# Gate and value products of the second expert by seven half-block products in fp16, in two passes over the tokens

## The chip, the cores and the metric

One core of a Trainium2 chip runs the whole program. The metric is device time in microseconds (us) of one execution, the median over executions. TensorE (PE) multiplies, VectorE (DVE), ScalarE (ACT) and GpSimd (POOL) do elementwise work, and the queue of SyncE (SP) issues nearly all DMAs.

## The reference

```python
def _moe2_ref(x, w_gate, w_val, w_out, rms_g):      # x: 2304 x 512
    rms = np.sqrt(np.mean(x * x, axis=-1, keepdims=True) + 1e-06)
    xn = x / rms * rms_g
    g = xn @ w_gate                                  # 512 x 1536
    silu = g * (1.0 / (1.0 + np.exp(-g)))
    val = xn @ w_val                                 # 512 x 1536
    return (silu * val @ w_out).astype(np.float32)   # 1536 x 512
...
attn_out = _attn_ref(**attn_kwargs)                  # block-causal, 4 batches, 8 heads, 576 x 64
x = attn_out.transpose(0, 2, 1, 3).reshape(B * S, H * D)
x = _moe_ref(x=x, **moe_kwargs)                      # softplus(x @ w_in) @ w_out, hidden 2048
return _moe2_ref(x=x, **moe2_kwargs)
```

## The kernel before

The 2304 tokens are cut into six blocks of 384 (`BLK`), features stand on the partitions. Every operand of a large product is held as a high and a low part in fp32r (a four-byte type), and each product is three matmuls (`PASSES`: high-high, high-low, low-high) that add up in one PSUM bank.

The program has three stretches. In the first (to about 406 us) attention runs together with nine of the sixteen hidden tiles of the first expert (`s_tile`, `pv`, `g1`, `g2`). Attention's probabilities are turned by DMA transposes (`pt<-pst`) that the SP queue issues; `pv` multiplies them in fp16. In the second stretch (to about 584 us) the other seven hidden tiles of each block run (`g1`, `g2`, `evac_b`), while the weights of the second expert are prepared. The third stretch is the second expert: 6 blocks by 12 hidden tiles of 128, which the text calls 72 f-steps. `g34` makes the gate and the value tile of one f-step, each from 12 matmuls of 128 x 384; the sigmoid, two multiplications and a split into high and low part follow on ACT and DVE; `g5`, one f-step later, multiplies the result by the output weights, 9 matmuls of 128 x 512. `out2` copies out a finished block, and `load_xn` normalises the next.

Weights come as 64-bit words. `w_unit` loads 512 KB (`wraw`), rebuilds fp32 values in `wa` by two ACT, three DVE and one POOL instruction per half, and splits them into `w`. Eleven of the 18 second-expert units are prepared in the second stretch, seven at the start of the third.

Nothing of the order is written by hand. Each operation is recorded with an engine, a cost, a priority and its cells; `Plan.schedule` simulates the engines, picks the operation with the lowest key among those ready, chooses between engines where `op2` offers several, and the result is emitted as one fixed order per engine. PE records matmuls in the helper `mm` (L422), so groups of PE are told apart by tiles: `b<-x,w` is `g1` or `g34`, `b<-g,w` is `g2`, `b<-w,g` is `g5`.

## Time and profile before

| | |
|---|---|
| time, median of 3 | 1040.66 us (1040.28 to 1041.27) |
| profiled execution's span, first to last instruction | 1038.3 us |
| what lies around the span, against the median | 2.4 us |
| PE busy | 1009.9 us, 97% of the span |
| DVE, ACT, POOL busy | 667.8, 580.1, 214.0 us |
| second expert's products | from about 584 us to 1033.7 us |

The time of the profiled execution itself is not given, so its span is set beside the median. A busy share is an average over the three stretches; the stretches differ, and what an edit is worth is read from its own.

### The profile page before, as it was taken

Reading aid. Unit: us, or ns where it says so; the run is one execution under the profiler, and the core shown is the slowest. Engines: PE = TensorE matmul, PEld = TensorE weight load, DVE = VectorE, ACT = ScalarE, POOL = GpSimd, SP = SyncE. Lnnn points to the kernel's source line nnn. Section 1 sums busy time; section 2 is a strip of 40 time slices with the busy share of each in tenths; the row PEclk is TensorE's granted clock in tenths of the full one; section 3 lists DMA queues with packets and bytes.
Section 4 is the critical chain, followed back from the end, with each engine's and each line's share of the span. In section 5 each row is a group of like instructions: output and inputs, shape, how many; then the busy total and the mean of one; then the engine's idle time right before and its main releaser. Section 6 shows DMA issues by size and latency. Waiting matters only on the chain.

```text
span 1038.3 us, 16885 instructions
## 1 busy us (share of the span) xinstructions
PE 1009.9 (97%) x6136; PEld 941.9 (91%) x6136; DVE 667.8 (64%) x1592; ACT 580.1 (56%) x1352; POOL 214.0 (21%) x289
## 2 busy tenths in 40 slices
PE   5999899999999999999999999999999999999998
PEld 4677898999989999999999999999999999999997
DVE  6899999887888677777888899422422423222322
ACT  6999798777778678877878664211211212111111
POOL 3543433331233023223324342000000000000000
PEclk9999999999999999999999999999999999999999
DMA  7454787958556635456444634200100100000000
GB/s 263 133 194 150 191 196 167 252 116 201 130 132 117 111 102 183 164 209 212 162 158 159 199 102 142 69 1 1 62 1 1 62 1 1 31 1 1 31 1 31
DMA packets 111635, 115.19 MB, mean 111 GB/s; under 512 B 84544, under 2 KB 92352, under 8 KB 110528
## 3 DMA queue, kind: packets, MB, share of 16 engines
q1 hardware_dynamic: 110976, 107.83, 36.8%
q0 software_dynamic: 576, 6.29, 1.6%
q8 instruction: 48, 0.79, 0.3%
q14 instruction: 35, 0.29, 0.1%
HBM read 72.03 MB, written 21.63 MB: 90 GB/s over the span
## 4 chain that ended last, share of the span: by engine, by line
PE 73%; DVE 9%; ACT 8%; DMA 7%; issue 2%; POOL 1%; SPq 0%; POOLq 0%; ACTq 0%; DVEq 0%
PE b L422 73%; DMA pt<-pst 4%; DMA wraw<-in_w_dram 2%; ACT P L661 1%; POOL wa L461 1%; ACT wa L448 1%; DVE wa L456 1%; DVE g L337 1%; ACT w L327 1%; DVE nm L627 1%; DVE wa L458 1%; DVE pst L686 1%; DVE t L836 1%; ACT t L834 1%; ACT P L705 1%
## 5 line engine op out<-in xcount | busy, mean ns | idle before, releaser
L422 PE MATMUL b<-x,w 128*128 128x384 f32 x2880 | 543.6, 338 | 2.0 <-DVE nm L669 0.8
L422 PEld LDWEIGHTS b<-x,w 128*128 128x128 f32 x2880 | 503.8, 188 | 13.8 <-issue 1.3
L422 PE MATMUL b<-g,w 128*128 128x384 f32 x1152 | 229.8, 339 | 2.2 <-DVE g L337 1.9
L422 PEld LDWEIGHTS b<-g,w 128*128 128x128 f32 x1152 | 199.4, 188 | 6.5 <-DVE g L337 3.6
L422 PE MATMUL b<-w,g 128*128 128x512 f32 x648 | 160.4, 392 | 0.0
L932 DVE TENSOR_TENSOR t<-b,t 128x384 f32<-128x384 f32 x72 | 40.0, 556 | 165.3 <-ACT t L931 165.1
L422 PEld LDWEIGHTS b<-w,g 128*128 128x128 f32 x648 | 120.6, 188 | 21.8
L461 POOL TENSOR_TENSOR wa<-wa,wraw 128x512 int32<-128x512 int32 x68 | 95.2, 1401 | 204.0 <-DVE wa L456 119.1
L931 ACT ACTIVATE t<-b 128x384 f32<-128x384 f32 x72 | 35.2, 490 | 171.8 <-PE b L422 171.8
L934 ACT CAST g<-t 128x384 fp32r<-128x384 f32 x72 | 36.8, 513 | 136.4 <-DVE t L933 136.4
L661 ACT ACTIVATE P<-b,nm 128x288 f32<-128x288 f32 (+8 forms) x160 | 80.1, 502 | 16.3 <-DVE nm L639 4.5
L627 DVE TENSOR_REDUCE nm<-b 128x1 f32<-128x288 f32 (+8 forms) x160 | 70.7, 447 | 18.7 <-PE b L422 17.6
L933 DVE TENSOR_TENSOR t<-b,t 128x384 f32<-128x384 f32 x72 | 39.9, 556 | 61.5 <-PE b L422 61.5
L686 DVE SCALAR_TENSOR_TENSOR pst<-P,nm,pst 128x128 f16<-128x128 f32 (+4 forms) x108 | 68.3, 638 | 9.1 <-ACT pst L683 6.7
L422 PE MATMUL b<-khl,qbd 128*128 128x448 f32 (+7 forms) x360 | 68.9, 312 | 1.0 <-ACT pt L722 1.0
L337 DVE TENSOR_TENSOR g<-t,g 128x384 fp32r<-128x384 f32 x96 | 60.5, 632 | 11.4 <-ACT g L327 10.9
L836 DVE SCALAR_TENSOR_TENSOR t<-b,t 128x384 f32<-128x384 f32 x96 | 52.6, 551 | 21.4 <-ACT t L835 21.0
L935 DVE TENSOR_TENSOR g<-t,g 128x384 fp32r<-128x384 f32 x72 | 42.9, 597 | 35.4 <-ACT g L934 35.4
L422 PEld LDWEIGHTS b<-khl,qbd 128*128 128x128 f32 x360 | 57.1, 188 | 3.9 <-ACT pt L722 1.2
L327 ACT CAST g<-t 128x384 fp32r<-128x384 f32 x96 | 49.2, 516 | 19.9 <-DVE t L836 16.8
L448 ACT ACTIVATE wa<-wraw 128x512 f32<-128x512 f32 x68 | 46.1, 678 | 20.9 <-DMA wraw<-in_w2gv_dram 10.7
L833 ACT ACTIVATE t<-b 128x384 f32<-128x384 f32 x96 | 46.5, 493 | 19.1 <-PE b L422 19.0
(91 smaller groups left out, 1055.7 us busy)
## 6 DMA issues: line engine op xcount, KB each, us to landing
wraw<-in_w_dram SPq DMA_DIRECT2D x32, 512.0 KB, 3.6
wraw<-in_w2gv_dram SPq DMA_DIRECT2D x24, 512.0 KB, 3.6
yd<-y SPq DMA_DIRECT2D x12, 768.0 KB, 3.7
y<-yd SPq DMA_DIRECT2D x12, 768.0 KB, 4.5
qf<-in_qP_dram SPq DMA_DIRECT2D x42, 192.0 KB, 2.8
xd<-x SPq DMA_DIRECT2D x4, 1536.0 KB, 7.1
x<-xd POOLq DMA_DIRECT2D x4, 1536.0 KB, 7.4
wraw<-in_w2o_dram SPq DMA_DIRECT2D x12, 512.0 KB, 4.4
```

The costliest lines, as they stand in the source:

```text
L327: "ACT": ("ACT", t_act(n), lambda: nc.scalar.copy(dst(), src())),
L337: "DVE": ("DVE", t_dve(n), lambda: nc.vector.tensor_tensor(dst(), a(), b(), ALU.subtract)),
L422: nc.tensor.matmul(o, lhsT=l, rhs=r, start=start, stop=stop)
L448: op("ACT", t_act(CW), prio, lambda a=a, hv=halves: nc.scalar.activation(a(), hv()[1].bitcast(FP32), ACTF.Abs), [raw], [a])
L461: op("POOL", t_pool2(CW), prio, lambda a=a, hv=halves: nc.gpsimd.tensor_tensor(a().bitcast(I32), a().bitcast(I32), hv()[0].bitcast(I32), A ...
L627: aop("DVE", t_dve(cn), key, lambda sp=sp, col=col, cn=cn: nc.vector.tensor_reduce(nm()[:, col:col + 1], sp()[:, :cn], axis=AX.X, op=ALU.m ...
L661: aop("ACT", 0.24 + cn * 0.836e-3, key, lambda sp=sp, col=col, c0=c0, cn=cn: nc.scalar.activation(P()[:, c0:c0 + cn], sp()[:, :cn], ACTF.E ...
L686: aop("DVE", t_dve(c, True), key, lambda: nc.vector.scalar_tensor_tensor(lo(), pc(), r(), hi(), ALU.mult, ALU.subtract), [P, (P, "pad"), ( ...
L833: op("ACT", t_act(BLK, False), key - 5, lambda: nc.scalar.activation(e(), h()[:, :BLK], ACTF.Abs), [h], [e])
L836: op("DVE", t_dve(BLK), key - 5, lambda: nc.vector.scalar_tensor_tensor(e(), h()[:, :BLK], 0.0, e(), ALU.max, ALU.add), [h, e], [e])
L932: op("DVE", t_dve(BLK), key + 2, lambda: nc.vector.tensor_tensor(u(), ga()[:, :BLK], u(), ALU.mult), [ga, u], [u])
L935: op("DVE", t_dve(BLK), key + 4, lambda: nc.vector.tensor_tensor(g()[:, 1], u(), g()[:, 0].bitcast(FP32), ALU.subtract), [u, (g, 0)], [(g, ...
```

## The change

The gate and value weights of two hidden tiles and the two token halves of a block are taken as two by two blocks: the 512 input features in halves, the 384 tokens in halves of 192 (`HB`). Seven products of sums of blocks (Strassen's scheme) replace the eight of the plain form; all operands are scaled and split into fp16 parts. A pair-step is what two f-steps were: 7 products of 12 matmuls 128 x 192, then 18 output matmuls of 128 x 512. There are 36. Silu is computed in one ACT instruction. Four of six pair-steps of every block run in a first pass (`SPL`), whose sums are stored in DRAM (`acc_dram`) with the seven mixed token blocks (`xn_dram`); a second pass runs the other two and adds. Scales need the largest weight, so `top_unit` loads all weights once more and takes a maximum on DVE: 24 halves of gate and value during attention, 12 of the output weights in the second stretch.

```diff
-    NW2 = NF2 + NF2 // 2
+    HB = 192
+    NP2 = NF2 // 2
+    NW2 = NF2 + NF2 // 4
...
+    def top_unit(i, key, prio):
+        for c in range(2):
+            raw = R_wraw.new()
+            hw = raw_pair(raw)[1]
+            load(prio - 6, raw, w_src[key[0]][key[1], c], writes=[raw], nbytes=128 * CW * 8)
+            op("DVE", t_dve(CW), prio, lambda k=2 * i + c, hw=hw: nc.vector.tensor_reduce(top(k), hw().bitcast(FP32), axis=AX.X, op=ALU.max, apply_absolute_value=True), [raw] + ([fac_b] if i >= NF2 else []), [("tops", 2 * i + c)])
...
+    def split_w(dst, src, n, r, rd, cells, prio):
+
+        op("ACT", t_act(n) + 0.09, prio, lambda: nc.scalar.activation(dst(0), src(), ACTF.Copy, scale=fac(r)), rd, [cells[0]])
+        op("DVE", t_dve(n, True), prio, lambda: nc.vector.scalar_tensor_tensor(dst(1), src(), fac(r), dst(0), ALU.mult, ALU.subtract), rd + [cells[0]], [cells[1]], port=True)
+
+    def gv_unit(f, ring, prio):
...
+        split_w(lambda l: dst(l, 0, 256).rearrange("p (k n) -> p k n", k=2), lambda: gp(0), 256, 0, [(g, 0)] + fc, [(w, 0, 0), (w, 1, 0)], prio)
+        split_w(lambda l: dst(l, 256, 768), lambda: fl()[:, 512:], 512, 0, [(g, 1)] + fc, [(w, 0, 1), (w, 1, 1)], prio)
+        for o, a, b in ((0, 1, 0), (1, 3, 1), (3, 3, 0), (2, 2, 3)):
...
+        split_w(lambda l: dst(l, 768, 1792), fl, 1024, 0, [(g, 0), (g, 1)] + fc, [(w, 0, 2), (w, 1, 2)], prio)
...
+        split_x(2, a22, hi_c, q(3))
+        mix(a22, a21, a22, ALU.add, lo_c + hi_c + q(3), q(3))
+        split_x(0, a11, lo_c, q(0))
+        split_x(3, a22, q(3), q(3))
+        mix(a21, a11, a21, ALU.subtract, lo_c + q(0, 3), q(2))
+        mix(a11, a22, a11, ALU.subtract, q(0, 2, 3), q(0))
+        split_x(1, a12, hi_c, q(1))
+        split_x(5, a21, q(2), q(2))
+        split_x(4, a11, q(0), q(0))
+        mix(a12, a12, a11, ALU.subtract, q(0, 1), q(1))
+        split_x(6, a12, q(1), q(1))
...
-                    for k in (2 * c, 2 * c + 1):
-                        for m, (a, l) in enumerate(PASSES):
-                            mm(o()[:, :BLK], w_view(w)[:, a, (k * 2 + q) * 128:(k * 2 + q + 1) * 128], x()[:, k, l, :], k == 0 and m == 0, k == KD - 1 and m == 2)
...
+                for f in range(2):
+                    for k in range(2):
+                        for m, (a, c) in enumerate(PASSES):
+                            mm(o()[:, HB * f:HB * f + HB], gv_w(ws[f], a, wsl, k), xn_view(x)[:, c, xs, k], first and f == 0 and k == 0 and m == 0, f == 1 and k == 1 and m == 2, skip_group_check=True)
...
+        for p, o, s in ((1, A, s1), (5, Bb, s5), (7, C, s7)):
+            product(p, o, True, False)
+            op("ACT", t_act(BLK, False), key + 1, lambda o=o, s=s: nc.scalar.copy(s(), ps(o)()), [o], [s])
+        product(6, D, True, True)
+        product(2, A, False, True)
+        product(3, Bb, False, True)
+        product(4, C, False, True)
...
+    steps = [(j, f, 0, SPL) for j in order for f in range(SPL)] + [(j, f, SPL, NP2) for j in ahead for f in range(SPL, NP2)]
...
+            if i0 == 0 and f == i0 + 1:
+                if j not in order[-2:]:
+                    spill_xn(j, key)
+                if j != order[-1]:
+                    load_xn(order[order.index(j) + 1], key)
+            if i0 and f == i0 and 0 < ahead.index(j) < NB - 1:
+                reload_xn(ahead[ahead.index(j) + 1], key)
```

Three places of the resulting order matter. The first is PE where f-steps or pair-steps follow each other. Before, in the steady third stretch, gate and value products in groups of 12 or 6 alternate with the three output banks:

```order
L422 MATMUL b_7936<-x,w 128x384 x12
L422 MATMUL b_7955<-x,w 128x384 x12
L422 MATMUL b_7978<-x,w 128x384 x6
L422 MATMUL b_7774<-w,g 128x512 x3
L422 MATMUL b_7783<-w,g 128x512 x3
L422 MATMUL b_7789<-w,g 128x512 x3
L422 MATMUL b_7978<-x,w 128x384 x6
```

In the changed program, this is PE where the first expert's last products and the first pair-step meet:

```order
L438 LDWEIGHTS w
L438 MATMUL b_7698<-x,w 128x192
L438 MATMUL b_7437<-g,w 128x384 x3
L438 MATMUL b_7442<-g,w 128x384 x3
L438 MATMUL b_7461<-g,w 128x384 x3
L438 LDWEIGHTS w
L438 MATMUL b_7738<-x,w 128x192
```

A matmul of 384 columns became one of 192 with an explicit weight load ahead of each, and the first pair-step's products are threaded between the last `g2` products.

The second place is DVE at the start of the second expert. Before, the gate multiplications (L932, L933), the split of `g` (L935) and the weight work on `wa` alternate:

```order
L933 TENSOR_TENSOR t<-b_7654,t 128x384
L933 TENSOR_TENSOR t<-b_7677,t 128x384
L932 TENSOR_TENSOR t<-b_7618,t 128x384
L913 SCALAR_TENSOR_TENSOR y<-y,gvec,r 128x384
L935 TENSOR_TENSOR g<-t,g 128x384 x2
L933 TENSOR_TENSOR t<-b_7702,t 128x384
L458 TENSOR_SCALAR wa<-wa 128x512 x2
L452 TENSOR_SCALAR wa<-wa 128x512
L935 TENSOR_TENSOR g<-t,g 128x384
```

In the changed program, at the same place, L1093 adds a PSUM bank to a stored product, L1017 is `evac_b`, L551 is the low part of a weight split and L341 a difference of weight blocks:

```order
L468 SCALAR_TENSOR_TENSOR wa<-wraw,wa 128x512
L1093 TENSOR_TENSOR m<-b_7794,m 128x384
L1017 TENSOR_TENSOR y<-b_7437,y 128x384
L341 TENSOR_TENSOR wg<-wg 128x2x128
L1017 TENSOR_TENSOR y<-b_7442,y 128x384
L1017 TENSOR_TENSOR y<-b_7461,y 128x384
L1017 TENSOR_TENSOR y<-b_7494,y 128x384
L1093 TENSOR_TENSOR m<-b_7777,m 128x384
L551 SCALAR_TENSOR_TENSOR w<-wg,fac,w 128x1024
L551 SCALAR_TENSOR_TENSOR w<-wa,fac,w 128x512
```

Weight splits of up to 1024 columns now stand between the additions that free the PSUM banks.

The third place is DVE during attention in the changed program, where L757 and L816 are the row maximum and the split of attention's probabilities and L510 is the new maximum over weights:

```order
L816 SCALAR_TENSOR_TENSOR pst<-P,nm,pst 128x3x128
L757 TENSOR_REDUCE nm<-b_1746 128x1
L800 RECIPROCAL nm<-nm 128x1
L799 TENSOR_SCALAR nm<-nm 128x1
L510 TENSOR_REDUCE tops<-wraw 128x1
L800 RECIPROCAL nm<-nm 128x1
L757 TENSOR_REDUCE nm<-b_1783 128x1
L799 TENSOR_SCALAR nm<-nm 128x1
```

L510 is new there; it waits for a 512 KB load that the SP queue issues among attention's transposes.

## Rows read from the trace of the kernel before

**Rows 1.** The page: busy time by engine; PE's granted clock in 40 slices.

```profile
PE 1009.9 (97%) x6136; PEld 941.9 (91%) x6136; DVE 667.8 (64%) x1592; ACT 580.1 (56%) x1352; POOL 214.0 (21%) x289
...
PEclk9999999999999999999999999999999999999999
```

**Rows 2.** Waits of PE, whole span: total us, times, longest.

```profile
PE b L422 <- DMA qf<-in_qP_dram: 4.4, 1, 4.4
PE b L422 <- DMA pt<-pst: 2.9, 5, 0.9
PE b L422 <- DVE g L337: 1.9, 3, 1.2
```

**Rows 3.** Stretches: length, busy PE, PEld, DVE, ACT, POOL; clock; DMA share, GB/s.

```profile
142.00:198.00 56.00, 55.03 (x447) 50.68 (x446) 50.88 (x155) 44.48 (x115) 18.70 (x33) 1.00 0.82 192
198.00:279.00 81.00, 81.00 (x604) 76.97 (x603) 68.27 (x198) 64.71 (x173) 21.62 (x42) 1.00 0.66 153
279.00:345.00 66.00, 63.37 (x524) 58.56 (x523) 57.66 (x190) 53.26 (x148) 18.41 (x40) 1.00 0.66 134
579.70:655.80 76.10, 76.02 (x402) 71.26 (x401) 67.57 (x117) 41.19 (x78) 25.30 (x18) 1.00 0.44 143
660.00:1000.00 340.00, 340.00 (x1791) 318.94 (x1791) 106.43 (x193) 65.11 (x131) 0.00 (x0) 1.00 0.05 17
```

**Rows 4.** PE in order of time, 1018 to 1034 us: start, length, count.

```profile
1018.91 4.35 PE L422 MATMUL b<-x,w 128*128 128x384 f32 x24
1023.10 2.24 PE L422 MATMUL b<-w,g 128*128 128x512 f32 x9
1025.17 4.35 PE L422 MATMUL b<-x,w 128*128 128x384 f32 x24
1029.36 4.30 PE L422 MATMUL b<-w,g 128*128 128x512 f32 x18
```

**Rows 5.** PE in order of time, 343.45 to 343.95 us, attention's fp16 products.

```profile
343.25 0.91 PE L422 MATMUL b<-pt,vhl 128*64 128x192 f16 x18
```

**Rows 6.** Groups by shape in that window: busy us, mean ns of one.

```profile
L422 PE MATMUL b<-pt,vhl 128*64 128x192 f16 x18 | 0.9, 246 | 0.0
```

**Rows 7.** Weight loads in order of time near 189.7 us, attention's fp32r products of 192 columns.

```profile
189.64 0.19 PEld L422 LDWEIGHTS b<-khl,qbd 128*128 128x128 f32 x1
189.75 0.19 PEld L422 LDWEIGHTS b<-x,w 128*128 128x128 f32 x1
```

**Rows 8.** DVE groups by shape, 579.7 to 655.8 us: busy, mean ns, idle before.

```profile
L456 DVE SCALAR_TENSOR_TENSOR wa<-wraw,wa 128x512 uint32<-128x512 uint32 x14 | 11.3, 810 | 0.1
L935 DVE TENSOR_TENSOR g<-t,g 128x384 fp32r<-128x384 f32 x12 | 9.5, 796 | 1.1 <-ACT g L934 1.1
L337 DVE TENSOR_TENSOR w<-wa,w 128x512 fp32r<-128x512 f32 x10 | 7.8, 784 | 0.2 <-ACT w L327 0.2
L932 DVE TENSOR_TENSOR t<-b,t 128x384 f32<-128x384 f32 x12 | 6.5, 548 | 2.5 <-ACT t L931 2.5
L452 DVE TENSOR_SCALAR wa<-wa 128x512 uint32<-128x512 uint32 x14 | 5.8, 417 | 0.0
```

**Rows 9.** DVE and ACT groups by shape, 660 to 1000 us.

```profile
L935 DVE TENSOR_TENSOR g<-t,g 128x384 fp32r<-128x384 f32 x55 | 30.7, 557 | 31.1 <-ACT g L934 31.1
L934 ACT CAST g<-t 128x384 fp32r<-128x384 f32 x55 | 28.2, 513 | 116.7 <-DVE t L933 116.7
L931 ACT ACTIVATE t<-b 128x384 f32<-128x384 f32 x54 | 26.5, 492 | 152.2 <-PE b L422 152.2
```

**Rows 10.** DVE groups by shape, 100 to 345 us: a maximum over 512 columns.

```profile
L627 DVE TENSOR_REDUCE nm<-b 128x1 f32<-128x512 f32 x11 | 7.5, 685 | 1.3 <-PE b L422 1.0
```

**Rows 11.** The page's DMA issues: count, KB each, median us to landing.

```profile
wraw<-in_w_dram SPq DMA_DIRECT2D x32, 512.0 KB, 3.6
...
x<-xd POOLq DMA_DIRECT2D x4, 1536.0 KB, 7.4
```

More of the change, by code (lines that the diff above doesn't have):

```diff
@@ L951, in out2 @@
[L951 to L960 removed]
+                for f in range(2):
+                    for m, (a, c) in enumerate(PASSES):
+                        mm(o[t](), u_view(u)[:, a, f, t * 128:(t + 1) * 128], o_view(w, wi)[:, c, f], i == i0 and f == 0 and m == 0, i == i1 - 1 and f == 1 and m == 2)
@@ new lines, in g5, with stage, out2 @@
+            op("PE", 6 * t_mmh(512), key, prod, [(w, wi, l, f) for l in range(2) for f in range(2)] + [(u, h, l) for h in range(2) for l in range(2)], [o[t]], cols=t_mm16(6 * 512))
+    def stage(t):
+        s = R_wa.new() if t < 2 else R_wraw.new()
+        return s, (s if t < 2 else lambda: s().bitcast(FP32)[:, 0:512])
+    def out2(j, key, last):
+        for t, o in enumerate(o_p.pop(j)):
+            s, v = stage(t)
+            r0 = j * BLK + t * 128
+            if last:
+                load(key - 8, v, acc_dram[j][:, t], reads=[("acd", j, t)], writes=[s], nbytes=262144)
+                op("DVE", t_dve(512, True), key, lambda v=v, o=o: nc.vector.scalar_tensor_tensor(v(), o(), fac(4), v(), ALU.mult, ALU.add), [o, ("f", 4), s], [s])
+                op("SP", 0.45, key, lambda v=v, r0=r0: nc.sync.dma_start(out=out[r0:r0 + 128, :], in_=v()), [s], [], done=1.0, nbytes=262144)
+                continue
+            op("ACT", t_act(512, False) + 0.09, key, lambda v=v, o=o: nc.scalar.activation(v(), o(), ACTF.Copy, scale=fac(4)), [o, ("f", 4)], [s])
+            op("SP", 0.45, key, lambda v=v, t=t: nc.sync.dma_start(out=acc_dram[j][:, t], in_=v()), [s], [("acd", j, t)], done=1.0, nbytes=262144)
@@ L963, in cost, with xn_cells, spill_xn, reload_xn @@
+    def xn_cells(x):
+        return [(x, i, l) for i in range(7) for l in range(2)]
+    def spill_xn(j, key):
+        x = x_b[j]
+        op("SP", 0.45, key, lambda: nc.sync.dma_start(out=xn_dram[j], in_=half(x)[:, 0:2 * 7 * 2 * HB]), xn_cells(x), [("xnd", j)], done=1.0, nbytes=1376256)
+    def reload_xn(j, key):
+        x = x_b[j] = R_x.new()
+        load(key, lambda: half(x)[:, 0:2 * 7 * 2 * HB], xn_dram[j], reads=[("xnd", j)], writes=xn_cells(x), nbytes=1376256)
     def cost(t):
@@ L1087 @@
     t_2 = key_b(n_b + LAG)
-    step2 = 24 * t_mm(BLK) + 9 * t_mm(512)
-    for i, kf in enumerate(w2[free_b + NA:]):
-        w_unit(kf, R_wB, t_2 + i * 4.0)
-    steps = [(j, f) for j in order for f in range(NF2)]
+    step2 = 84 * t_mmh(HB) + 18 * t_mmh(512)
+    SPL = 4
+    late = w2[free_b + NA:]
+    w2_unit(late[0], R_wB, t_2 - 8)
+    ahead = [order[-1], order[-2]] + order[:-2]
+    steps = [(j, f, 0, SPL) for j in order for f in range(SPL)] + [(j, f, SPL, NP2) for j in ahead for f in range(SPL, NP2)]
     LAG = 1
```

283 lines of the change are left out of this document (209 added, 74 removed).

## The prediction

> **What bounds the kernel now.** I read the busy times first: PE is busy for 97% of the span and its granted clock stays at full speed, the 2.4 GHz level, throughout [rows 1]. The list of PE's waits agrees: outside the start the longest is 0.9 us, and all waits for attention's transposes together are 2.9 us [rows 2]. So the time is the sum of PE's matmuls, and an edit that takes matmul time away pays in full, unless another engine then fails to keep up. For that I read the busy times by stretch: in the steady second expert DVE is busy for 106 of 340 us and ACT for 65, but at its start, from 579.7 to 655.8 us, DVE is busy for 67.6 of 76.1 us while PE still does not wait [rows 3]. During attention DVE is full as well: 50.9 of 56, 68.3 of 81 and 57.7 of 66 us [rows 3]. These are the two places where a faster PE or more DVE work can bite.
>
> **The products, before.** An f-step is 33 matmuls: 24 of 384 columns and 9 of 512. In order of time 24 start at 1018.91 and the next group at 1023.10, so 174.6 ns each; the 9 take until 1025.17, 230 ns each [rows 4]. That makes 6.26 us; 1791 matmuls in 340 us, 33 to an f-step, give 6.265 [rows 3]. 72 f-steps are 451.1 us.
>
> **The products, after.** A pair-step is 84 matmuls of 192 columns and 18 of 512, all fp16, each with its own weight load. No row shows such a product over the full array. The nearest is attention's: fp16, 192 columns, weights of 64 columns, two matmuls side by side in the two halves of the array. 18 of them, 9 pairs, take 0.91 us from the first start to the last end [rows 5], one lasts 246 ns [rows 6], so a pair starts every (910 - 246) / 8 = 83 ns, and two loads of 64 columns, 128 together, have passed in that time. This is my price for 192 columns: 83 ns, which is 192 columns at 2.4 GHz (80 ns) and 3 more. For 512 columns the same law gives 213.3 + 3 = 216.3 ns; the fp32r row's 230 is the upper end. A pair-step is then 84 x 83 + 18 x 216.3 = 6972 + 3893 ns = 10.87 us, 36 are 391.1 us, and the gain is 451.1 - 391.1 = **60 us**. By the upper end for 512 columns it is 51.
>
> The other bound for 192 columns is the weight load. Attention's fp32r products of the same 192 columns load 128 columns each, and their loads start 110 ns apart (189.64, 189.75), though the columns alone would need 80 [rows 7]: there the load sets the pace. If a full fp16 load costs as much, the gain is gone (a rival, below). I take 83, because the fp16 row is of the same type and already carries 128 weight columns in the time of one matmul.
>
> The Trainium skill speaks against this value: "TensorE: Matmul & The Clock Gate", section "Back-to-back issue gap", puts a stream of weight load and matmul pairs at about 81 ns for 128 columns, where a lone matmul would take about 56. Read as 25 ns of load on top of each matmul, an estimate from that page, the 84 products would take 9.07 us and the gain would turn into a loss of 16 us; this case's attention row [rows 5] does not show such an addition, but its loads are half as wide.
>
> **The start of the second expert.** DVE's order after the change has 61 instructions from the last softplus to the end of the first pair-step: 9 that read PSUM, 24 of 384 columns in SBUF, 12 cheap scalar ones, 6 sign merges, 5 weight splits of 512 columns, one of 1024, and four small. By the means of this stretch before (548, 796, about 430, 810, 784 ns and in proportion [rows 8]) they sum to some 41.5 us. The records overlap a little: 117 instructions filled 67.57 us, 0.58 each [rows 3], which for 61 would be 35. At the quiet price of an SBUF instruction, 557 ns [rows 9], I get 29. I take 37, since POOL is adding weights beside DVE there again and the mix is wider. PE's order puts 48 old matmuls (8.4 us) and 17 groups of 12 new ones (16.8 us) ahead of the first output product that needs this result: 25 us. PE therefore stands still for about 12 us, bounded by 4 (29) and by 16 (37 with DVE's own idle share, 8.5 of 76.1 us). Its later steps in the first pass each bring 5.1 us of DVE work, a quarter of a block's 8.6 us of mixing and splitting and a quarter of a weight unit of about 7: some 9 of 10.87 us, hidden but without much margin; I add 1. **+13 us**.
>
> **Attention.** 24 maxima over 512 columns at 685 ns [rows 10] are 16.4 us, and DVE has 5 + 13 + 8 = 26 us idle in 203 us [rows 3], so they fit. Each waits for a 512 KB load of 3.6 us [rows 11] in DVE's fixed order, and the load passes through the SP queue and the DMA engines (66 to 82% busy [rows 3]) together with the transposes. What is late then is a transpose, and PE. Bounds: nothing, and 24 times the longest transpose wait, 0.9 us [rows 2], 21.6. I take the size of the waits that PE has already, **+3 us**.
>
> **The end.** Behind the last product stand seven DVE instructions (4 us) and a Silu and a cast (0.5 each [rows 9]) with 18 output matmuls, 3.9 us, as cover: **+1 us**.
>
> **At nothing.** ACT gains three copies and has two Silu and two casts per pair-step, seven at about 0.5 us [rows 9], 3.5 of 10.8 us, hidden behind PE. The reloads in the second pass (1.4 MB; 1.5 MB took 7.4 us [rows 11]) have a block of 21.6 us each, and DMA is 5% busy there [rows 3]; uncovered, four of them would cost 30. In the second stretch weight work on DVE grows, but POOL takes over squares' sums and norms; the last block has 52 DVE instructions where it had 50.
>
> **Sum.** The traced execution has a span of 1038.3 us, and the median of the runs is 2.4 above it; I keep that distance. 1040.7 - 60 + 13 + 3 + 1 = **998 us**.
>
> **The rivals.** First, DVE sets the pace through the whole first pass. Its order has 272 instructions up to the fourteenth pair-step, where PE stands at about 175 us after the last softplus, the 12 us of idling included. At 0.58 each they take 158 and fit; by the full means of rows 8, without the overlap, they sum to about 196. Then the stall is 13 + 21 = 34 us and the time 1019. For it speaks that DVE was 89% busy at this place with less to do [rows 3]; against it that POOL works less once the weights are done, and SBUF instructions go back to 557 ns [rows 9].
>
> Second, the loads of the maxima hold back attention: 21.6 instead of 3 us, 1016. Against it: the planner spreads 24 loads over more than 200 us.
>
> Third, and slower than before: the weight load sets PE's pace. At 110 ns [rows 7] 84 products take 9.24 us, a pair-step 13.13, and 36 take 472.8, 21.7 more than the 451.1 of today. With DVE's stall cut to about 8 and the other 4 the time is 1074. It decides from the point where 36 x 84 x (p - 83 ns) eats 60 - 17 = 43 us, at p = 97 ns. For it speaks the fp32r row, against it the fp16 row [rows 5]. The rule of the Trainium skill named above would, by its 25 ns, land at 1040.7 + 16 + 12 = 1069.
>
> Fourth, no stall at all: only the lower bounds, 1040.7 - 60 + 4 = 985 or less.
>
> **How the numbers follow.** The forecast with its bounds (985 to 1010, the likeliest's own range) 0.64; DVE through the first pass, around 1019, 0.18; attention, around 1016, 0.06; the load, by either price 1050 and above, 0.10; no stall, below 985, 0.02. The range 984 to 1024 leaves out the load and the last, about 0.12, and a little of the second case. 0.2% is 2 us, about what a measurement of this kernel can tell from no change. All cases but the load are faster: 0.89; within 0.2% 0.01; slower 0.10.
>
> **What would show it.** In the profile after: 3024 matmuls of 128 x 192 that start 82 to 84 ns apart, and 648 of 512 at about 216; a steady pair-step of 10.9 us in the second pass; idle time of PE between roughly 580 and 620 us that ends with DVE, some 12 us; waits for `pt<-pst` of a few us more than 2.9. I am wrong if the 192-column products are more than 95 ns apart, if PE goes on waiting for DVE in every step of the first pass, if PE waits for a `wraw` load or a maximum before 400 us by more than 10 us, or if the reloads of the second pass show up as waits of PE.

## The result, and the profile after

The changed kernel takes 1015.09 us (median of five runs, 1012.0 to 1021.46) against 1040.66 (1039.96 to 1041.31) before: a ratio of 0.9758, interval 0.9728 to 0.9788, faster. The forecast was 998, within 984 to 1024: the gain is 25.6 us where 42.7 were forecast. The profiled execution is the slowest of the five, 1021.46 us with a span of 1019.7, so the profile below has some 6 us more loss to show than the median.

The page first, busy time by engine and the granted clock in 40 slices. Against [rows 1] PE has 43 us less to do in a span only 19 us shorter, DVE 132 us more, and the clock is below full in slices 24 and 26, where the second expert starts.

```profile
PE 966.8 (95%) x7438; PEld 841.0 (82%) x7438; DVE 799.8 (78%) x1819; ACT 658.2 (65%) x1491; POOL 277.3 (27%) x353
...
PEclk9999999999999999999999989899999999999999
```

**The products.** PE in order of time at the end of the second pass, then the page's row for the weight loads (how many, busy us, mean ns of one):

```profile
1000.55 7.09 PE L438 MATMUL b<-x,w 128*128 128x192 f16 x84
1007.48 7.93 PE L438 MATMUL b<-w,g 128*128 128x512 f16 x36
```

```profile
L438 PEld LDWEIGHTS <-w 128*128 128x128 f16 x3024 | 252.7, 98 | 22.8 <-issue 14.1
```

84 products start within 1007.48 - 1000.55 = 6.93 us, 82.5 ns each; 36 matmuls of 512 columns take (7.93 - 0.38) / 35 = 215.7 ns each. A pair-step is 6.93 + 18 x 0.2157 = 10.81 us, 36 are 389.3, and the products gain 451.1 - 389.3 = 61.8 us. A load of 128 fp16 columns lasts 98 ns, longer than that spacing, and adds nothing to it that can be seen: 192 columns at the 2.4 GHz level are 80 of the 82.5 ns.

**The stretches.** Length, busy PE, PEld, DVE, ACT, POOL; clock; DMA share, GB/s. The first three are those of [rows 3]; then the start of the second expert and the steady rest.

```profile
142.00:198.00 56.00, 50.30 (x367) 45.10 (x366) 45.58 (x128) 36.87 (x94) 14.39 (x27) 0.94 1.02 230
198.00:279.00 81.00, 77.23 (x558) 72.44 (x557) 70.56 (x211) 62.67 (x167) 22.64 (x45) 1.00 0.94 247
279.00:345.00 66.00, 66.00 (x548) 61.69 (x548) 58.42 (x190) 53.73 (x149) 22.64 (x46) 1.00 0.64 156
660.00:1000.00 340.00, 340.00 (x3198) 272.40 (x3196) 234.58 (x413) 158.36 (x306) 43.07 (x36) 1.00 0.27 93
...
100.00:200.00 100.00, 90.50 (x669) 81.65 (x667) 86.08 (x271) 68.80 (x190) 33.27 (x61) 0.96 0.94 222
580.00:660.00 80.00, 62.03 (x455) 52.21 (x454) 74.08 (x114) 51.12 (x98) 37.56 (x30) 0.89 0.40 140
```

From 660 to 1000 us PE is busy without a gap, though DVE has 235 of 340 us where it had 106. Two places lose. In attention, where DMA was 82 and 66% busy [rows 3], it is now at 102% and 94% (packet times against 16 engines, so the figure can pass 100), and PE is idle for 5.7 and 3.8 us where it was idle for 1.0 and 0; the clock's mean of 0.94 in the first of these stretches is worth up to 3.4 us more. Only the third stretch gains, from 2.6 us of idle time to none. Between 580 and 660 us PE is idle for 18.0 us (before: 0.1 in 76 [rows 3]) and the clock's mean is 0.89.

To keep the two apart I use one mark: the start of the 54th softplus (L836 before, L966 after), the last one that attention runs beside. The first 54 of them, before and after, with the starts of the first and the last:

```profile
L836 DVE SCALAR_TENSOR_TENSOR t<-b,t x54: 536/548/559, 54.9 to 397.1; 128x384 f32<-128x384 f32 x54
L966 DVE SCALAR_TENSOR_TENSOR t<-b,t x54: 529/551/559, 56.7 to 411.2; 128x384 f32<-128x384 f32 x54
```

Before it is at 397.1 us, after at 411.2, a lag of 14.1. The lags of the ten softplus on either side lie between 12.6 and 17.2, so the split between the two places is good to some 3 us. From it to the end of the last product pass 636.5 us before (to 1029.36 + 4.30) and 604.2 after (to 1007.48 + 7.93). That is 32.3 less where the products give 61.8, so 29.5 are lost at the start: 18.0 of idle time, up to 8.8 of clock (0.11 of 80 us), and about 3 not assigned.

PE's waits in two stretches, 100 to 300 us and 580 to 655 us: total us, times, longest.

```profile
PE b L438 <- ACT P L791: 6.5, 5, 2.8
PE b L438 <- DMA pt<-pst: 3.1, 2, 1.8
...
PE b L438 <- ACT m L1106: 6.1, 3, 5.1
PE b L438 <- ACT x L1051: 2.9, 1, 2.9
PE b L438 <- DVE m L1093: 2.8, 1, 2.8
```

Two of these gaps in order of time: start us, length us, engine, and in brackets the idle time before. The first is the 2.8 us before 620.80, with DVE and POOL beside it; the second the 5.1 us before 638.85, with ACT and one line of DVE.

```profile
616.52 1.73 POOL L475 TENSOR_TENSOR wa<-wa,wraw 128x512 int32<-128x512 int32 x1
616.76 1.24 PE L438 MATMUL b<-x,w 128*128 128x192 f16 x13
...
617.03 1.51 DVE L464 TENSOR_SCALAR wa<-wa 128x512 uint32<-128x512 uint32 x1
618.22 1.18 POOL L1095 TENSOR_TENSOR m<-m 128x384 f32<-128x384 f32 x1
...
618.46 1.21 DVE L341 TENSOR_TENSOR wg<-wg 128x256 f32<-128x256 f32 x1
...
620.20 0.55 DVE L1093 TENSOR_TENSOR m<-b,m 128x384 f32<-128x384 f32 x1
620.80 0.56 PE L438 MATMUL b<-x,w 128*128 128x192 f16 x3 [2.80 <-DVE m L1093]
```

```profile
631.56 0.52 ACT L1030 ACTIVATE r<-r 128x384 f32<-128x384 f32 x1 [2.34 <-DVE r L1029]
...
632.66 1.28 ACT L1115 ACT_TABLE_LOAD   x1
...
636.90 0.72 ACT L550 ACTIVATE w<-wg,fac 128x512 f16<-128x512 f32 x1
...
637.51 0.51 ACT L1130 CAST g<-t 128x384 f16<-128x384 f32 x1
637.91 0.52 ACT L1130 CAST g<-m 128x384 f16<-128x384 f32 x1
...
638.32 0.85 ACT L1106 COPY m<-b 128x384 f32<-128x384 f32 x2
...
638.52 1.08 DVE L1131 TENSOR_TENSOR g<-m,g 128x384 f16<-128x384 f32 x1
...
638.85 0.64 PE L438 MATMUL b<-x,w 128*128 128x192 f16 x3 [5.13 <-ACT m L1106]
```

PE waits for a PSUM bank each time. In the first gap L1093, which frees it, stands in DVE's order behind weight work: a shift (L464), which took 417 ns on average in the kernel before [rows 8], takes 1.51 us while POOL's L475 runs, and a difference (L341) takes 1.21 beside POOL's L1095. In the second the bank is freed by ACT's copy L1106, and it is ACT's order that holds it: from 631.56, when DVE's L1029 released it, to that copy ACT is busy without a pause, with norms, a record ACT_TABLE_LOAD of 1.28 us, three Silu, weight work and two casts. DVE is hardly earlier: the first output product also needs L1131, which ends at 639.60, and that product starts at 640.73.

The same split, L551 with `w<-wa,fac,w` of 512 columns, under two different POOL instructions:

```profile
608.92 1.49 POOL L475 TENSOR_TENSOR wa<-wa,wraw 128x512 int32<-128x512 int32 x1 [5.88 <-ACT m L1106]
609.18 1.78 DVE L551 SCALAR_TENSOR_TENSOR w<-wa,fac,w 128x512 f16<-128x512 f32 x1
...
625.46 1.69 POOL L1011 TENSOR_TENSOR r<-r,t 128x384 f32<-128x384 f32 x1 [2.21 <-ACT t L1022]
626.21 1.49 DVE L551 SCALAR_TENSOR_TENSOR w<-wa,fac,w 128x512 f16<-128x512 f32 x1
```

Both end 0.55 us after the POOL instruction, and so do all eight of this split in the trace that start under one, whether they take 1.05 or 1.78 us; the four others take 0.74.

The Trainium skill, "SBUF — State Buffer", section "SBUF: two separate sides", describes the port pair that GpSimd and VectorE share as a lock: where a DVE instruction has two SBUF inputs, or runs in a mode that uses both ports, whichever of the two engines starts first holds the pair for its whole instruction. The trace agrees: L551 ends at a fixed distance from POOL's end and not from its own start, the shift of the first gap ends 0.29 us after L475 (618.25, 618.54), and L1093, which reads a PSUM bank, keeps its 0.55 beside POOL.

The clock: PE in order of time behind the second gap, and the granted clock of that stretch (columns as above).

```profile
638.85 2.08 PE L438 MATMUL b<-x,w 128*128 128x192 f16 x12 [5.13 <-ACT m L1106]
640.73 5.63 PE L438 MATMUL b<-w,g 128*128 128x512 f16 x16
```

```profile
639.00:644.60 5.60, 5.60 (x22) 2.94 (x21) 5.60 (x10) 3.70 (x7) 2.22 (x3) 0.50 0.05 20
```

Twelve products take 640.73 - 638.85 = 1.88 us, 157 ns each and not 82.5: PE runs at the 1.2 GHz level, right behind 5 us in which it stood still.

### The profile page after: what moved, and what is told of

It reads as the page before. It is cut to its first block, busy times and chain, and to the rows that moved or that the text cites. A ratio compares the mean times of both kernels' runs of the same rounds, so it can differ in the third digit from the quotient of the medians.

```text
span 1019.7 us, 20047 instructions
## 1 busy us (share of the span) xinstructions
PE 966.8 (95%) x7438; PEld 841.0 (82%) x7438; DVE 799.8 (78%) x1819; ACT 658.2 (65%) x1491; POOL 277.3 (27%) x353
## 4 chain that ended last, share of the span: by engine, by line
PE 73%; DVE 10%; DMA 8%; ACT 6%; issue 2%; SPq 0%; POOL 0%; ACTq 0%; DVEq 0%
PE b L438 73%; DMA wraw<-in_w2gv_dram 3%; DMA wraw<-in_w_dram 2%; DMA raw<-in_vP_dram 1%; DMA raw<-in_kT_dram 1%; DVE pst L816 1%; DVE nm L757 1%; ACT P L791 1%; DVE g L341 1%; DVE w L551 1%; ACT P L835 1%; DVE t L966 1%; DMA pt<-pst 1%; DVE wa L468 1%; DVE tops L510 1%
## 5 line engine op out<-in xcount | busy, mean ns | idle before, releaser
L438 PE MATMUL b<-x,w 128*128 128x192 f16 (+1 forms) x4176 | 491.9, 273 | 14.2 <-ACT m L1106 6.1
L438 PEld LDWEIGHTS <-w 128*128 128x128 f16 x3024 | 252.7, 98 | 22.8 <-issue 14.1
L438 PEld LDWEIGHTS b<-x,w 128*128 128x128 f32 x1152 | 199.6, 188 | 7.5 <-DVE nm L799 1.2
L438 PE MATMUL b<-w,g 128*128 128x512 f16 x648 | 147.6, 383 | 0.0
L438 PEld LDWEIGHTS <-g 128*128 128x128 f16 x648 | 63.4, 99 | 69.7 <-issue 2.4
L1106 ACT COPY m<-b 128x384 f32<-128x384 f32 x108 | 51.2, 477 | 81.9 <-PE b L438 81.7
L791 ACT ACTIVATE P<-b,nm 128x288 f32<-128x288 f32 (+8 forms) x160 | 79.7, 500 | 27.8 <-DVE nm L757 7.3
L1095 DVE TENSOR_TENSOR m<-m 128x384 f32<-128x384 f32 x64 | 37.9, 592 | 68.9 <-ACT m L1106 68.2
L475 POOL TENSOR_TENSOR wa<-wa,wraw 128x512 int32<-128x512 int32 x44 | 63.8, 1450 | 88.9 <-DVE wa L468 51.7
L757 DVE TENSOR_REDUCE nm<-b 128x1 f32<-128x288 f32 (+8 forms) x160 | 70.6, 449 | 16.1 <-PE b L438 14.2
L341 DVE TENSOR_TENSOR g<-t,g 128x384 fp32r<-128x384 f32 x96 | 65.5, 684 | 8.5 <-ACT g L331 8.2
L816 DVE SCALAR_TENSOR_TENSOR pst<-P,nm,pst 128x128 f16<-128x128 f32 (+4 forms) x108 | 66.3, 626 | 3.3 <-ACT pst L813 2.5
L966 DVE SCALAR_TENSOR_TENSOR t<-b,t 128x384 f32<-128x384 f32 x96 | 52.7, 551 | 18.0 <-ACT t L965 17.6
L331 ACT CAST g<-t 128x384 fp32r<-128x384 f32 x96 | 48.9, 513 | 14.5 <-DVE t L966 11.1
L475 POOL TENSOR_TENSOR wg<-wg,wraw 128x512 int32<-128x512 int32 x24 | 34.3, 1431 | 87.3 <-DVE wg L468 67.0
L964 ACT ACTIVATE t<-t 128x384 f32<-128x384 f32 x96 | 50.4, 528 | 1.4
L965 ACT ACTIVATE t<-t 128x384 f32<-128x384 f32 x96 | 50.3, 527 | 1.2
```

What stands on the lines that cost most here:

```text
L331: "ACT": ("ACT", t_act(n), lambda: nc.scalar.copy(dst(), src())),
L341: "DVE": ("DVE", t_dve(n), lambda: nc.vector.tensor_tensor(dst(), a(), b(), ALU.subtract)),
L438: nc.tensor.matmul(o, lhsT=l, rhs=r, start=start, stop=stop, **kw)
L475: op("POOL", t_pool2(CW), prio, lambda: nc.gpsimd.tensor_tensor(a().bitcast(I32), a().bitcast(I32), lw().bitcast(I32), ALU.add), [cell, (r ...
L757: aop("DVE", t_dve(cn), key, lambda sp=sp, col=col, cn=cn: nc.vector.tensor_reduce(nm()[:, col:col + 1], sp()[:, :cn], axis=AX.X, op=ALU.m ...
L791: aop("ACT", 0.24 + cn * 0.836e-3, key, lambda sp=sp, col=col, c0=c0, cn=cn: nc.scalar.activation(P()[:, c0:c0 + cn], sp()[:, :cn], ACTF.E ...
```

## The experiments

Each variant is planned anew, so beside the edit the whole order shifts a little. In this table "lag" is that of the 54th softplus, "rest" the time from it to the end of the last product, and idle and clock are PE's between 580 and 660 us; these four are from one execution each, the profiled one.

| run | us (range) | ratio to before, interval | lag | rest | idle | clock |
|---|---|---|---|---|---|---|
| the change | 1015.1 (1012.0 to 1021.5) | 0.9758, 0.9728 to 0.9788 | 14.1 | 604.2 | 18.0 | 0.89 |
| e1_no_maxima | 1003.7 (1002.9 to 1005.4) | 0.9654, 0.9640 to 0.9669 | 1.6 | 598.5 | 14.3 | 0.89 |
| e2_loads_only | 1020.7 (1019.7 to 1024.1) | 0.9826, 0.9805 to 0.9848 | 11.9 | 604.5 | 16.9 | 0.89 |
| e3_reduces_only | 1007.0 (1005.5 to 1008.0) | 0.9682, 0.9668 to 0.9697 | 0.1 | 602.5 | 15.6 | 0.91 |
| e4_no_pool_add | 995.3 (991.2 to 996.6) | 0.9564, 0.9541 to 0.9587 | 9.8 | 583.9 | 3.8 | 0.98 |
| e5_later_maxima | 1013.8 (1010.5 to 1016.8) | 0.9740, 0.9712 to 0.9767 | 11.1 | 599.0 | 12.1 | 0.87 |
| e6_earlier_weights | 1020.0 (1015.9 to 1024.6) | 0.9801, 0.9766 to 0.9836 | 16.2 | 605.5 | 19.3 | 0.91 |
| e7_filler | 1025.0 (1022.4 to 1027.8) | 0.9849, 0.9824 to 0.9874 | 10.4 | 614.3 | 11.7 | 0.91 |
| e8_three_together | 999.2 (997.8 to 1006.7) | 0.9621, 0.9576 to 0.9665 | 9.6 | 586.4 | 6.7 | 0.96 |
| e9_held_loads | 1012.3 (1010.9 to 1013.0) | 0.9725, 0.9704 to 0.9746 | 6.6 | 602.6 | 17.0 | 0.89 |
| e10_add_aside | 1028.7 (1026.6 to 1032.5) | 0.9894, 0.9859 to 0.9929 | 20.6 | 603.5 | 11.8 | 0.96 |
| e11_or_on_dve | 1002.8 (993.7 to 1005.1) | 0.9618, 0.9570 to 0.9667 | 5.4 | 593.6 | 6.9 | 0.96 |
| e12_or_and_held | 995.4 (992.2 to 995.9) | 0.9567, 0.9553 to 0.9580 | 10.0 | 583.0 | 3.5 | 0.98 |

### Attention: the loads or the maxima

**e1_no_maxima.** A constant stands for the 24 maxima.

```diff
-    for i, kf in enumerate(tk[:NF2]):
-        top_unit(i, kf, win[1] + (win[NB - 1] - win[1]) * i / NF2)
+    op("DVE", 0.1, win[NB - 1] - 6, lambda: nc.vector.memset(tops[:, 4:28], 1.6), [], [("tops", i) for i in range(2 * NF2)])
```

> The changed kernel without the 24 loads and 24 DVE maxima of the gate and value weights during attention; a constant stands in their place. Theory (the maxima's loads hold back attention): the softplus of the 54th f-step, 14 us later than before in the changed kernel's trace, comes back to within 3 us of before, and the time falls by 8 to 14 us, to about 1003. Rival (attention was lost to something else, such as the new order itself): the lag stays near 14 us and the time near 1015. The stall of PE between 580 and 640 us stays in both, 15 to 20 us.

**e2_loads_only.** The loads stay, nothing reads them; a constant stands for the maxima.

```diff
-        top_unit(i, kf, win[1] + (win[NB - 1] - win[1]) * i / NF2)
+        for c in range(2):
+            load(win[1] + (win[NB - 1] - win[1]) * i / NF2 - 6, raw_ := R_wraw.new(), w2gv[i, c], writes=[raw_], nbytes=128 * CW * 8)
+    op("DVE", 0.1, win[NB - 1] - 6, lambda: nc.vector.memset(tops[:, 4:28], 1.6), [], [("tops", i) for i in range(2 * NF2)])
```

> As the one before, but the 24 loads of 512 KB stay and only the DVE maxima are left out (a constant stands in their place). If the DMA engines and the SP queue are what holds attention back: the DMA share between 100 and 200 us stays above 0.9, the lag at the 54th softplus stays 7 us or more, time about 1008 to 1015. If it is DVE's wait for each load and the 16 us of work: lag below 4 us, time about 1003 as without both.

**e3_reduces_only.** The 24 maxima read a weight tile of the first expert that is in SBUF anyway, there are no loads, and a constant replaces the result.

```diff
-        top_unit(i, kf, win[1] + (win[NB - 1] - win[1]) * i / NF2)
+    w_res = w_units["w1", 0]
+    for i in range(2 * NF2):
+        op("DVE", t_dve(CW), win[1] + (win[NB - 1] - win[1]) * (i // 2) / NF2, lambda i=i: nc.vector.tensor_reduce(top(i), w_res()[:, 0, 0].bitcast(FP32), axis=AX.X, op=ALU.max, apply_absolute_value=True), [(w_res, 0, 0)], [("tops", i)])
+    op("DVE", 0.1, win[NB - 1] - 6, lambda: nc.vector.memset(tops[:, 4:28], 1.6), [], [("tops", i) for i in range(2 * NF2)])
```

> The 24 DVE maxima stay, but read a weight tile that lies in SBUF already, and the 24 loads are left out (a constant replaces the result). If DMA holds attention back: lag at the 54th softplus below 4 us, time about 1003. If DVE's 16 us of extra work does it: lag 7 us or more, time 1008 to 1015.

The stretch from 100 to 200 us in these three runs, in this order (columns as above), and the landing time of attention's transposes from 100 to 300 us: in the change, then in e1 (count, us).

```profile
100.00:200.00 100.00, 96.88 (x745) 87.93 (x746) 89.97 (x289) 79.75 (x215) 37.69 (x65) 0.97 0.71 181
```

```profile
100.00:200.00 100.00, 90.26 (x666) 81.79 (x667) 82.03 (x258) 71.10 (x190) 32.41 (x58) 0.93 0.98 265
```

```profile
100.00:200.00 100.00, 97.81 (x751) 89.61 (x752) 93.09 (x302) 79.47 (x217) 39.29 (x66) 0.97 0.76 185
```

```profile
pt<-pst SPq DMA_TRANSPOSE x24, 6.3
```

```profile
pt<-pst SPq DMA_TRANSPOSE x26, 4.9
```

With the loads and no maxima the lag stays (11.9); with the maxima and no loads it is gone (0.1), although DVE is then busy for 93.1 of these 100 us, more than in the change. So DVE's 16 us of maxima are hidden in attention, as forecast (in the whole, e3 is 3.2 us slower than e1, by intervals that just touch), and the 24 loads of 512 KB are not. e2's time, 1020.7, lies above both of its ranges and above the change's: with nothing reading them, all 24 loads fall between 100 and 200 us, where the change has 16.

How the loads hold attention back is shown in part. They fill the DMA engines, and attention's transposes land later (6.3 us against 4.9). But SP's queue, which issues both in a fixed order, also stands still for them: between 100 and 300 us it waits 7.9 us for maxima (L510) to free a buffer in the change, and 9.0 us for earlier loads in e2, and what is behind such a load is issued later. And in the change DVE, too, stands still in its order for such loads, 6.2 us ahead of L510. e1 and e3 take away all of this at once, so the shares stay open.

### Attention: spreading the loads

**e5_later_maxima** starts them at a later block, **e9_held_loads** plans each load behind a matmul group of the first expert.

```diff
-        top_unit(i, kf, win[1] + (win[NB - 1] - win[1]) * i / NF2)
+        top_unit(i, kf, win[3] + (win[NB - 1] - win[3]) * i / NF2)
```

> The 24 loads for the maxima of the gate and value weights are spread over the time from the fourth block of attention on, instead of from the second on; nothing is left out. Theory (the loads are late for attention only because they run on the DMA engines where its weights' loads and transposes are densest): the DMA engines' share in 100 to 200 us falls from 0.94 to below 0.85, the lag of the 54th softplus behind the kernel before falls from 14 us to 6 us or less, and the time to 1005 to 1010 us. Rival (the bytes cost the same wherever they stand in attention): lag stays at 12 to 15 us, time 1013 to 1019 us.

```diff
-    def top_unit(i, key, prio):
+    def top_unit(i, key, prio, after=((), ())):
...
-            load(prio - 6, raw, w_src[key[0]][key[1], c], writes=[raw], nbytes=128 * CW * 8)
+            load(prio - 6, raw, w_src[key[0]][key[1], c], writes=[raw], nbytes=128 * CW * 8, after=after[c])
...
-        top_unit(i, kf, win[1] + (win[NB - 1] - win[1]) * i / NF2)
+        top_unit(i, kf, win[1] + (win[NB - 1] - win[1]) * i / NF2, [[g1_op[steps[8 + (2 * i + c) * 36 // (2 * NF2)]]] for c in range(2)])
```

> Each of the 24 loads for the gate and value maxima is planned behind one matmul group of the first expert, so that they are issued one by one over attention (eighth to forty-fourth hidden-tile step, about 110 to 345 us) and not as soon as a buffer is free; nothing is left out. Theory (attention is held up because loads and transposes crowd the DMA engines between 100 and 280 us): the DMA engines' share in 100 to 200 us falls from 0.94 to 0.85 or less, the lag of the 54th softplus from 14 us to 3 to 8 us, the time to 1003 to 1010 us. Rival (every 512 KB costs attention the same wherever it stands): lag 11 us or more, time 1012 to 1018 us.

The loads issued from 100 to 200 us in the change, in e5 and in e9 (count, KB, us to landing), and that stretch in e9:

```profile
wraw<-in_w2gv_dram SPq DMA_DIRECT2D x16, 512.0 KB, 4.9
```

```profile
wraw<-in_w2gv_dram SPq DMA_DIRECT2D x18, 512.0 KB, 4.7
```

```profile
wraw<-in_w2gv_dram SPq DMA_DIRECT2D x9, 512.0 KB, 6.2
```

```profile
100.00:200.00 100.00, 97.28 (x760) 89.45 (x761) 92.64 (x301) 76.89 (x211) 39.53 (x70) 0.97 0.86 214
```

e5 did not do what it was for: a load has a key, but it is issued whenever the queue and a buffer are free, and 18 instead of 16 fell into that stretch. It tells nothing of the theory. e9 did: 9 loads there, PE busy for 97.3 of 100 us instead of 90.5, and a lag of 6.6. The lag is that of its theory, but the time, 1012.3, is that of its rival and not separated from the change's (the intervals overlap), and the lag does not follow the spread alone: e11 below, with 16 early loads, has 5.4 and e12, with held ones, 10.0. What stands is the difference between all the loads and none; what decides between a lag of 5 and one of 16 stays open.

### The start: POOL beside DVE

**e4_no_pool_add.** POOL's addition of the lowest bits (L475) is left out for the second expert's weights, 36 instructions of 68 (not the 44 told of below), so those bits are missing from them.

```diff
-        op("POOL", t_pool2(CW), prio, lambda: nc.gpsimd.tensor_tensor(a().bitcast(I32), a().bitcast(I32), lw().bitcast(I32), ALU.add), [cell, (raw, "l")], [cell])
+        if low:
+            op("POOL", t_pool2(CW), prio, lambda: nc.gpsimd.tensor_tensor(a().bitcast(I32), a().bitcast(I32), lw().bitcast(I32), ALU.add), [cell, (raw, "l")], [cell])
...
-            to_fp32(raw, lambda c=c: g()[:, c], (g, c), prio)
+            to_fp32(raw, lambda c=c: g()[:, c], (g, c), prio, False)
...
-                to_fp32(raw, a, a, prio)
+                to_fp32(raw, a, a, prio, False)
```

> The changed kernel without POOL's addition of the lowest weight bits for the second expert (44 instructions fewer, the bits are left out); DVE's instructions stay. Theory (DVE is the bound at the start of the second expert because its SBUF instructions take up to twice as long beside POOL): the DVE weight splits of 512 columns between 580 and 640 us fall from about 1300 to 700 ns, PE's idle time there from 17 us to 5 or less, the half clock goes with it, and the time falls by 12 to 22 us, to about 995 to 1003. Rival (DVE simply has too many instructions there): idle time stays above 12 us, the time within 5 us of 1015.

DVE's weight work from 580 to 640 us by shape (busy, mean ns), in the change, then in e4 (L552 is the change's L551):

```profile
L551 DVE SCALAR_TENSOR_TENSOR w<-wa,fac,w 128x512 f16<-128x512 f32 x6 | 7.8, 1295 | 0.0
...
L468 DVE SCALAR_TENSOR_TENSOR wg<-wraw,wg 128x512 uint32<-128x512 uint32 x4 | 3.6, 910 | 0.0
...
L464 DVE TENSOR_SCALAR wg<-wg 128x512 uint32<-128x512 uint32 x4 | 2.5, 629 | 0.0
```

```profile
L468 DVE SCALAR_TENSOR_TENSOR wg<-wraw,wg 128x512 uint32<-128x512 uint32 x4 | 2.7, 681 | 0.0
...
L464 DVE TENSOR_SCALAR wg<-wg 128x512 uint32<-128x512 uint32 x4 | 1.6, 415 | 0.0
L552 DVE SCALAR_TENSOR_TENSOR w<-wa,fac,w 128x512 f16<-128x512 f32 x2 | 1.5, 744 | 0.0
```

The rest falls by 20.3 us to 583.9, the idle time to 3.8, and the clock to within 2% of full. Two things went at once: more of DVE's instructions are quick, and the chain from load to split is shorter by POOL's instruction. The first can be sized. Between 580 and 660 us the DVE instructions that start under a running POOL instruction take 17.6 us more in the change than the same ones do beside none (worked out from the trace; 7.4 of it under L475, the rest under the norms, sums and differences that the planner gave to POOL). In the kernel before it is 12.3 us in this stretch, in e4 7.6. It does not decide by itself: e9 below has 12.7 us of it and 17.0 us of idle time.

**e10_add_aside.** To separate them, POOL's instruction stays for all weights but adds the low bits to themselves, so that nothing waits for it (the weights lack their lowest bits).

```diff
-        op("POOL", t_pool2(CW), prio, lambda: nc.gpsimd.tensor_tensor(a().bitcast(I32), a().bitcast(I32), lw().bitcast(I32), ALU.add), [cell, (raw, "l")], [cell])
+        op("POOL", t_pool2(CW), prio, lambda: nc.gpsimd.tensor_tensor(lw().bitcast(I32), lw().bitcast(I32), lw().bitcast(I32), ALU.add), [(raw, "l")], [(raw, "l2")])
```

> POOL's addition stays as an instruction of the same shape for all weights of both experts, but it adds the low bits to themselves in their own buffer, so that nothing waits for its result (this leaves the lowest bits out of the rebuilt weights). It separates the two things that the run without POOL's addition took away at once. Theory (DVE's instructions are slowed while POOL works): the slowing stays, PE idle between 580 and 655 us stays at 12 us or more, time 1008 to 1016 us. Rival (the chain through POOL, some 1.4 us a half, holds up the splits): idle 6 us or less, time 993 to 1000 us.

It does not separate them: 1028.7 lies outside both ranges. The first expert's weights were touched too, the lag is 20.6, PE idles for 7.5 us between 400 and 575 us, where the change has none, and the slowing moved to other instructions between 580 and 640 us (L472 on `wg` has a mean of 863 ns against 621 in the change, L551 on `wa` 745 against 1295). Which of the two weighs more stays open.

**e11_or_on_dve.** For the second expert's weights DVE puts the low bits in by an or, in the instruction that shifted before, and POOL has no part in it. The low bits are rounded down, which for weights below 2 in magnitude gives the same values but for the rounding.

```diff
+        def shift_or():
+            au = a().bitcast(U32)
+            nc.vector.scalar_tensor_tensor(au, au, 3, lw(), ALU.logical_shift_left, ALU.bitwise_or)
+        def sign_and():
+            au = a().bitcast(U32)
+            nc.vector.scalar_tensor_tensor(au, hw(), 0x3FFFFFFF, au, ALU.bitwise_or, ALU.bitwise_and)
...
-        op("ACT", t_act(CW), prio, lambda: nc.scalar.activation(lw().bitcast(I32), lw(), ACTF.Copy, scale=2.0**-29), [raw], [(raw, "l")])
+        op("ACT", t_act(CW), prio, lambda: nc.scalar.activation(lw().bitcast(I32), lw(), ACTF.Copy, bias=-0.5 if short else 0.0, scale=2.0**-29), [raw], [(raw, "l")])
...
+        if short:
+            op("DVE", t_dve(CW), prio, shift_or, [cell, (raw, "l")], [cell], port=True)
+            op("DVE", t_dve(CW), prio, sign_and, [cell, raw], [cell], port=True)
+            return
...
```

> For the second expert's weights the low bits are put in by DVE: the shift, a DVE instruction with one input, becomes one with two inputs that takes them in by an or (about 0.68 us in place of 0.42 us, 36 halves), the sign's mask changes to fit, ScalarE's low part is rounded down, and POOL's addition falls away; nothing is left out for weights below 2 in magnitude. Theory (POOL beside DVE, and the chain through it, made the start's loss): PE idle between 580 and 655 us 3 to 8 us, time 995 to 1003 us. Rival (DVE's amount of work is what counts there, and 9 us more of it in the whole, some 4 us at the start, eats the gain): idle 10 us or more, time 1006 to 1013 us.

1002.8 us, with 6.9 us of idle time: as the theory had it, though this order also waits 5.6 us between 400 and 575 us, 2.7 of them for the scale of the output weights. DVE's instruction became dearer (0.69 us where the shift alone takes 0.42) and the start still shorter, so DVE's work at its undisturbed prices is not what decides there. The four runs lie between 993.7 and 1005.1 us, and no run shows why they differ so.

### The start: amount and clock

**e6_earlier_weights** and **e7_filler**:

```diff
-        place.append(max([int(2 + i * (n_b - 4) / (free_b + NA))] + place[-1:] + [last.get(i - free_b, -9) + 3]))
+        place.append(max([int(2 + i * (n_b - 8) / (free_b + NA))] + place[-1:] + [last.get(i - free_b, -9) + 3]))
```

> The second expert's weight units are placed closer together in the second stretch, so that the last of them end some four first-expert steps sooner; nothing is left out. Theory (the start waits because more DVE work than fits stands between 580 and 640 us): work moved ahead of 580 us shortens PE's idle time there from 17.4 us to 8 to 12 us and the time by 5 to 12 us, to 1003 to 1010 us. Rival (the work only moves, and DVE or a buffer makes the second stretch wait instead, or the units still wait for their buffers): idle time stays within 2 us of 17.4 or the lag at the end of the second stretch grows by as much as the start gains; time 1012 to 1018 us.

```diff
+                if j == order[0] and i < 2:
+                    for z in range(24):
+                        mm(o()[:, 384:512], gv_w(ws[1], 0, wsl, 1), xn_view(x)[:, 0, xs, 1][:, 0:128], False, z == 23, skip_group_check=True)
```

> 24 further matmuls of 128 x 128 are issued behind each group of products in the first two pair-steps of the first block, into 128 columns of the bank that nothing reads; they add about 14 groups of 1.3 us to PE (18.6 us at full clock). Theory (the half clock between 585 and 645 us costs about 8.6 us by itself, and DVE's pace leaves PE 17 us of idle time there): the filler lies in idle time, the granted clock stays nearer to full, and the time falls by 3 to 8 us, to 1007 to 1012 us. Rival (PE only waits for DVE there, and the half clock is hidden behind the same wait): time within 2 us of 1015 us, with a higher clock; if the filler itself is on the path, up to 1025 us.

e6 moved nothing: DVE is busy for 62.6 us from 500 to 580 us, 63.1 in the change, and idle time and rest are as before. The earlier placement did not move the work, so the theory is not tested. e7 adds 336 matmuls that start 56 ns apart, 18.8 us, and the rest grows by 10.1: some 9 us lay in time that PE would have lost anyway (its idle time fell by 6.3), but the time as a whole rose. That the half clock costs by itself is seen in the spacing of 157 ns above, but whether the time would be waited for anyway, e7 does not tell.

### Together

**e8_three_together** takes e4 (without ACT's instruction for the low bits too, which leaves out the same bits), e5's loads and e6's placement with 10 for 8.

> Three edits in one: the second expert's weights are taken without POOL's addition of their lowest bits and without ScalarE's instruction that scales those bits (this leaves out the lowest bits of the rebuilt fp32 values), the maxima's loads are spread over attention's later blocks, and the weight units are placed closer together. Theory (attention's loss is the early loads, the start's loss is DVE slowed beside POOL and crowded): lag at the 54th softplus 6 us or less, PE idle between 580 and 655 us 4 us or less, time 980 to 990 us. Rival (each of these losses is paid elsewhere once it is taken away): 993 to 997 us, no better than the run without POOL's addition alone.

The rival held: 999.2 us, no better than e4 alone. Two of its three edits are those of e5 and e6, which did not do what they were for.

**e12_or_and_held** is e11 with e9's loads.

> The or on DVE for the second expert's weights (as in the run before) together with the held loads of the maxima; nothing is left out for weights below 2 in magnitude. If the two losses are separate and add up: lag at the 54th softplus 4 to 8 us, PE idle between 580 and 655 us 3 to 8 us, time 994 to 1000 us, below both kernels and below the or alone (1002.8 us). Rival (one gives back what the other brings, the plan being made anew): 1001 to 1006 us.

995.4 us, 4.3% below the kernel before (interval 4.2 to 4.5) and 2% below the change: the lowest median of those that leave nothing out but the rounding told of at e11, though not separated from e11's (the intervals overlap between 0.9570 and 0.9580). The start as it should be, columns as above:

```profile
580.00:660.00 80.00, 76.52 (x668) 63.48 (x667) 70.95 (x127) 50.88 (x101) 25.09 (x21) 0.98 0.42 137
```

But the two edits do not add up as expected: against e11 the lag went from 5.4 to 10.0, outside the 4 to 8 expected, and the whole gain is in the rest, 593.6 to 583.0. There PE's idle time between 400 and 575 us fell from 5.6 to 1.7 us, mostly since the order made anew no longer waits for the scale, and at the start from 6.9 to 3.5.

## Why the prediction was right, and where it was mis-sized

The time lies in the stated range and outside the likeliest one, 985 to 1010. The sign and the largest term came out by the mechanism that was forecast; the two losses were of the kinds that were named, and both larger.

**The products** were right: 83 and 216.3 ns forecast, 82.5 and 215.7 measured, 60 us against 61.8. The attention row with two half-width products [rows 5] carried over to full-width loads, and the fp32r row's 110 ns [rows 7] did not. The Trainium skill's rule ("TensorE: Matmul & The Clock Gate", "Back-to-back issue gap"), read as 25 ns of load on each matmul, is not borne out by the 82.5 ns.

**The start** was right in kind, idle time of PE behind DVE, and mis-sized: 13 against 29.5, beyond the 16 that bounded it. The idle time is 18.0, not 12. Of it 4.5 us lie before the last softplus (the 2.4 and 2.1 us of waits for the first expert's `g`, ACT L331 and DVE L341); my sum began at that softplus. The 13.5 behind it are near the forecast, but by luck, from two errors that offset each other. From the last softplus (598.16, L966) DVE needed 41.4 us to the end of the last instruction that the first output product waits for (639.60, L1131) where I took 37. The full means of [rows 8] gave 41.5, and I discounted them for overlap. Of the 41.4 some 11 are time that DVE's instructions under POOL's took beyond their price beside none (worked out from the trace), which leaves about the lower value that I had named, 29; the same rows summed again give some 31 for it. And PE's cover lasted 29.1 us (640.73 - 598.16 less 13.5) and not the 25 that I gave it, since part of it ran at the lower clock. That clock, up to 8.8 us, was no term at all: it was full in every stretch of [rows 3] that I read, where PE stood still for at most 2.6 of 66 us. Here the 0.50 stands behind 5.1 us of idle time, so a stall is dearer than its length. ACT, which I put at nothing, is hidden in the steady part and not here: its order ends the longest gap.

**Attention** was mis-sized, 3 against 14.1 in the profiled execution. Its upper bound, 21.6, held. I sized it by the waits that PE had already, on DMA engines that were 66 to 82% busy [rows 3]; 24 loads of 512 KB took them to 94 and 102%, and made SP's queue wait for buffers. The second rival's argument against it, that the loads are spread over 200 us, failed: they are issued as buffers come free, 16 of 24 between 100 and 200 us. What I expected to be late, the transposes, is not the larger part in the change: between 100 and 300 us PE's waits for them grew from 1.9 to 3.1 us, those behind attention's probabilities (`P`, L791 on ACT) from 0.3 to 6.5. In e2, without the maxima, it is the transposes, 7.6 us.

**The reloads, and ACT in the steady part,** at nothing: PE is busy for 340.00 of 340 us, as forecast. **The end,** 1 us forecast: behind the last product the span has 4.6 us before (1038.3 - 1033.7) and 4.3 after (1019.7 - 1015.4). **The rivals:** DVE pacing the whole first pass did not come (235 of 340 us); the weight load did not come; that the time lies near the second rival's 1016 is coincidence, two thirds of its 21.6 us and an undersized start. In the profiled execution the terms are -61.8 + 14.1 + 29.5 = -18.2, the last of them being what was left over, and the spans differ by 18.6.
